# A list-scheduled attention and MLP kernel: a shift on the due date of every step, and a new set of planner constants

## The chip, the cores and the metric

One core of one Trainium2 chip runs the whole program. The metric is the device time of one execution in microseconds (us). Five engines work beside each other, each through its own instructions in order: PE (TensorE, matmuls; its weight loads are listed as PEld), DVE (VectorE), ACT (ScalarE), POOL (GpSimd) and SP (SyncE, which here issues nearly all DMAs). They wait for one another on semaphores.

## The reference

```python
for t in range(S):                       # attention: r, k, v, w are (4, 8, 768, 48), u is (8, 48)
    cur = einsum('bhd,bhe->bhde', u[None] * kt, vt)
    y[:, :, t] = einsum('bhd,bhde->bhe', rt, state + cur)
    state = wt[:, :, :, None] * state + einsum('bhd,bhe->bhde', kt, vt)
x = y.transpose(0, 2, 1, 3).reshape(3072, 384)
h = maximum(maximum(x @ w1, x @ w2), x @ w3)        # 384 -> 768
x = h @ w_out                                       # 768 -> 384
g = x @ w_gate                                      # 384 -> 1536
out = (g / (1 + exp(-g))) * (x @ w_val) @ w_out2    # 1536 -> 384
```

All of it in fp32; the weights arrive as 64-bit floats, whose words the kernel turns into fp32 itself.

## The kernel before

**Units, chunks, chains.** The attention is cut into 24 *units*: 6 chunks of 128 time steps (`c`) by 4 groups of heads (`j`, in the order 3, 0, 1, 2). A unit n goes round the engines several times. DVE makes `rk` (L478), the suffix products `I` (L418), `kh` (L421, L423), the prefix products `F` (L431) and `rp` (L434). PE then does `rk_sum` (tile `pa`, L484), the transposes of `kh` (tile `kp`, L527), `scores` (`sc`, L513), `outer` (`sc`, L609), the two parts of `y` (L553, L566) and `take_upper` (L639); the last units of chunks 0, 1 and 5 also `lend` (L539). Between them ACT copies `kp` to `khT` (L531), fills the diagonal of `A` (L499), scales the first state (L618), copies the upper half `xh` of `y` (L630) and, after `take_upper`, the lower half `xl` (L648). DVE masks `sc` into `A` (`causal`, L518) and adds to the states `s` and `S` (L622, L445). The first chunk is units 0 to 3.

**Layers.** Four finished units are one chunk of tokens (512 columns). Its first MLP is 18 `up` steps (f = 0 to 5, m = 0 to 2), each a run of nine 128x512 matmuls (L663 to L665, tile `ps`): every fp32 product is made of three matmuls with the operands split into a high and a low part. DVE takes the maximum (L768). For chunk 0 the weights are prepared just ahead: a DMA brings the 64-bit words (`raw`), DVE makes fp32 words of them in three instructions (L169 to L171), ACT rounds the high part (`hi`, L732), DVE subtracts the low part (`lo`, L737). Six `down` steps follow; in chunk 0 they are plain fp32 matmuls of the whole words (L785, `ps<-hh,whole`), each step three of them. While PE does the layers of a chunk, the next chunk's units run in between.

**Second MLP.** Twelve units of 128 hidden features (n = 0 to 11, `NU`), each for three pairs of chunks: 30 `product` steps (three matmuls of tile `px` or `py`, L973) and, laid between them, the six projections of the unit before (`proj`, tile `po`, L663 to L665 once more, nine matmuls each). Before its first low-part matmul a projection waits for `pr` from DVE (`prod_low`, L1024). All projections but the last use one PSUM tile, which has to be emptied by `collect` (L1049 on DVE, L1044 on ACT) before the next may start. `snap` (ACT, L982), `join` (DVE, L987, L989) and `mix` (POOL, L997; for k = 5 L994, on DVE in the units that `MIX5` names) combine the products; `silu` (L1004), `gate_times` (L1007) and `prod_high` (L1021) make the gated values.

**What sets the order.** Every step is entered in a `Plan` with an engine, a cost, the steps that it depends on and a due date. `Plan.order` (L72) replays the program over these costs. It pulls each due date forward to what the followers need, and then, again and again, for each engine takes the step with the smallest key among those that could start within a window `win` of the earliest start. `wt` weighs the start against the due date, `stay` favours more of the same kind; in the first 85 us of the replay fixed values stand for the three:

```python
wt, win, stay = (TUNE["wt"], TUNE["win"], TUNE["stay"]) if best > 85.0 else (15.0, 0.3, 2.0)
...
t["key"] = t["due"] + wt * t["at"] - stay * (t["kind"] == last.get(t["eng"]))
```

The sequence that comes out is what each engine gets. The second MLP's sequence on PE is fixed apart from that by `seq`: the table `GAPS` says behind which product (v, i) each of the six projections stands, and `TUNE['gaps']` which table a unit uses: the first number for most units, the second for units 4 and 8, the third for units 1 to 3. The two tables that matter here are

```python
{(0, 10): 0, (0, 13): 1, (1, 8): 2, (1, 9): 3, (1, 11): 4, (1, 13): 5},    # GAPS[2]
{(0, 11): 0, (0, 14): 1, (1, 4): 2, (1, 7): 3, (1, 10): 4, (1, 12): 5},    # GAPS[6]
```

## Time and profile before

| | us |
|---|---|
| median of 3 runs (lowest, highest) | 806.79 (805.52, 811.22) |
| the profiled execution | 805.78 |
| its span, first to last instruction | 804.0 |
| PE busy in it | 783.2 (97%) |
| DVE busy | 624.0 (78%) |
| ACT busy | 451.4 (56%) |
| POOL busy | 286.1 (36%) |

The profile is of one execution. Busy times are shares of the span. A PE matmul of 512 columns is listed with about 0.39 us, but in a stream one starts every 0.227 us or so: they overlap, and their ends are modelled. So a short wait can lie hidden in a busy PE, and the start-to-start distance shows it. In a timeline the time of a merged row runs from its start to the end of its last instruction.

### The profile page before, as it was taken

The page shows a single profiled execution, that of the slowest core. Times are in us where ns is not written, and L with a number is a line of the kernel's source. Part 1 is how long each engine was busy: PE and PEld are TensorE (multiplying, and loading weights), DVE is VectorE, ACT ScalarE, POOL GpSimd, SP SyncE. Part 2 cuts the span into 40 slices and gives each one's busy share as a digit, 9 for nine tenths or more (in the row PEclk, how much of TensorE's full clock was granted, in tenths as well). Part 3 has the DMA queues.
Part 4 walks back from the last instruction along what each step waited for, and adds up shares of the span by engine and source line. Part 5 has one row for each costly group of instructions (what it writes and reads, how often), then busy time and mean ns, then how long its engine had stood idle before and what let it go on. Part 6 is the DMA issues. An engine that isn't in the chain of part 4 may idle for free.

```text
span 804.0 us, 15834 instructions
## 1 busy us (share of the span) xinstructions
PE 783.2 (97%) x6140; PEld 638.1 (79%) x6140; DVE 624.0 (78%) x930; ACT 451.4 (56%) x983; POOL 286.1 (36%) x281
## 2 busy tenths in 40 slices
PE   6899999999999999999999999999999999999997
PEld 5777668888888888888877877878888887888885
...
GB/s 275 184 214 186 148 166 168 195 253 120 166 244 161 189 208 99 175 260 371 229 315 145 165 222 280 234 325 276 242 298 217 288 274 209 244 160 229 92 1 82
DMA packets 46482, 167.02 MB, mean 208 GB/s; under 512 B 6048, under 2 KB 11040, under 8 KB 41152
## 3 DMA queue, kind: packets, MB, share of 16 engines
...
q10 hardware_dynamic: 144, 0.13, 0.1%
...
## 4 chain that ended last, share of the span: by engine, by line
PE 88%; DVE 6%; issue 2%; POOL 1%; ACT 1%; DMA 1%; DVEq 0%; ACTq 0%
PE px L973 14%; PE py L973 13%; PE ps L663 11%; PE ps L664 10%; PE ps L665 10%; PE po L663 6%; PE po L664 6%; PE po L665 6%; PE y L553 2%; PE ps L785 2%; PE kp L527 2%; PE sc L609 2%; PE sc L513 1%; PE pa L484 1%; PE y L566 1%
## 5 line engine op out<-in xcount | busy, mean ns | idle before, releaser
L973 PE MATMUL px<-yo,W 128*128 128x512 f32 x567 | 147.6, 390 | 0.4 <-DVE sb L987 0.3
L973 PE MATMUL py<-yo,W 128*128 128x512 f32 x498 | 130.4, 389 | 0.4 <-ACT sb L982 0.4
L663 PE MATMUL ps<-xh,hi 128*128 128x512 f32 x324 | 128.9, 398 | 0.0
L664 PE MATMUL ps<-xl,hi 128*128 128x512 f32 x324 | 126.4, 390 | 0.7 <-ACT xl L648 0.5
L665 PE MATMUL ps<-xh,lo 128*128 128x512 f32 x324 | 126.4, 390 | 0.1
L997 POOL TENSOR_TENSOR sb<-sb 128x512 f32<-128x512 f32 x46 | 61.0, 1327 | 181.9 <-ACT sb L982 160.3
L973 PEld LDWEIGHTS px<-yo,W 128*128 128x128 f32 x567 | 106.2, 188 | 23.5 <-DVE sb L987 1.5
L973 PEld LDWEIGHTS py<-yo,W 128*128 128x128 f32 x498 | 93.3, 188 | 20.2 <-ACT sb L982 0.8
L987 DVE TENSOR_TENSOR sb<-px,sb 128x512 f32<-128x512 f32 x95 | 64.0, 686 | 31.8 <-PE px L973 30.4
L663 PE MATMUL po<-pr,Wp 128*128 128x512 f32 x213 | 83.6, 393 | 0.5 <-DVE acc L1049 0.2
L664 PE MATMUL po<-pr,Wp 128*128 128x512 f32 x213 | 83.2, 390 | 0.4 <-DVE pr L1024 0.4
L665 PE MATMUL po<-pr,Wp 128*128 128x512 f32 x213 | 82.9, 389 | 0.0
L1021 ACT ACTIVATE pr<-pt 128x512 fp32r<-128x512 f32 x71 | 41.9, 598 | 59.0 <-DVE pt L1007 58.0
L427 POOL COPY total<-I 128x8 f32<-128x8 f32 x24 | 11.9, 495 | 171.2 <-DVE s L445 93.0
L665 PEld LDWEIGHTS ps<-xh,lo 128*128 128x128 f32 x324 | 60.8, 188 | 13.7 <-DVE lo L737 0.5
L982 ACT ACTIVATE sb<-px 128x512 f32<-128x512 f32 x96 | 56.3, 598 | 26.8 <-PE px L973 23.9
L664 PEld LDWEIGHTS ps<-xl,hi 128*128 128x128 f32 x324 | 60.9, 188 | 12.7 <-ACT xl L648 0.8
L663 PEld LDWEIGHTS ps<-xh,hi 128*128 128x128 f32 x324 | 60.8, 188 | 12.7 <-issue 0.2
L1049 DVE TENSOR_TENSOR acc<-po,acc 128x512 f32<-128x512 f32 x53 | 36.4, 688 | 34.6 <-PE po L665 33.7
L1004 ACT ACTIVATE pt<-sb 128x512 f32<-128x512 f32 x72 | 42.6, 603 | 27.4 <-DVE pr L1024 27.3
L768 DVE TENSOR_TENSOR hw<-hw,ps 128x512 f32<-128x512 f32 x60 | 40.6, 679 | 19.9 <-PE ps L665 12.6
L989 DVE TENSOR_TENSOR sb<-sb,py 128x512 f32<-128x512 f32 x47 | 32.2, 685 | 28.3 <-ACT sb L982 25.0
...
## 6 DMA issues: line engine op xcount, KB each, us to landing
...
```

Of the source, the lines that this page charges most:

```text
L663: nc.tensor.matmul(ps, lh, rh, start=first, stop=False)
L664: nc.tensor.matmul(ps, lh, rl, start=False, stop=False)
L665: nc.tensor.matmul(ps, ll, rh, start=False, stop=last)
L768: nc.vector.tensor_tensor(hws[f], hws[f], pss[c, f, m], ALU.max)
L973: nc.tensor.matmul(X[n, v, ch], w, x, start=first and k == 0, stop=k == 2, skip_group_check=True)
L982: nc.scalar.activation(sbuf(n, v, k), X[n, v, ch], AF.Copy)
L987: nc.vector.tensor_tensor(b, X[n, v, ch], b, ALU.add)
L989: nc.vector.tensor_tensor(b, b, X[n, v, ch], ALU.subtract)
L997: nc.gpsimd.tensor_tensor(b, b, buf[n, v, "u" if k == 3 else "d"], ALU.add)
L1004: nc.scalar.activation(gated[n, k], buf[n, 0, k], AF.Silu)
L1021: nc.scalar.activation(prod[n, k][:, 0, :], gated[n, k], AF.Copy)
L1049: nc.vector.tensor_tensor(acc[a], t, acc[a], ALU.add)
```

## The change

Three tables change and one line of the planner. Every step now has a name: the function with its integer and string arguments. `SHIFT` gives a number to 666 such names, mostly steps of the weight preparation, of the second MLP and of their DMAs; `EARLIER` gives one to 201 keys of `L`: steps of units 0 to 7 and of chunk 0's layers with their weights. The shift (from -44.8 to +31.1) is added to the due date in the key by which `order` chooses; it moves no step past what it depends on, and adds or removes no instruction. `TUNE` has new values for 23 constants. Among them `mix5` (0, 3) is now (3, 11): the k = 5 mix of unit 0 goes to POOL, that of unit 11 to DVE; and `gaps` (6, 2, 3) is now (6, 6, 3): units 4 and 8 use the last of the tables instead of the third.

```diff
+SHIFT = {('w_low', 3, 0, 0): -23.8, ('product', 1, 1, 6): -11.2, ('op_high', 1, 11): 17.9, ('snap', 3, 1, 0, 'B'): -4.7,
...
+EARLIER = {('rp', 1): 6.4, ('lv', 0): 2.5, ('hl', 0, 5): -18.8, ('la', 2): 12.4, ('state1', 5): -6.5, ('scores', 7): -25.5,
...
-TUNE = {'wt': 29.41, 'win': 0.99, 'stay': 0.74, 'period': 62.0, 'soon': 14.07, 'up5': -17.12, 'check': 29.53, 'bits': -7.63,
-  'u1': 380, 'u0': 370.17, 'prep': -36.51, 'xpre': 82.52, 'xgap': 7.97, 'xafter': 11.7, 't': -8.63, 'te': 2.5, 'p1': 354.2,
-  'p2': 397.32, 'p0': 14.36, 'p3': -2.49, 'slow': (3, 5, 6, 8, 10), 'op': -11.67, 'sums': -9.09, 'mix5': (0, 3),
-  'words2': 0.75, 'gaps': (6, 2, 3), 'collect': 6.42, 'v': 2.26}
+TUNE = {'wt': 32.67, 'win': 0.89, 'stay': 1.71, 'period': 62.6, 'soon': 14.07, 'up5': -17.12, 'check': 20.84, 'bits': -9.88,
+  'u1': 377.7, 'u0': 369.84, 'prep': -37.12, 'xpre': 80.34, 'xgap': 7.97, 'xafter': 11.56, 't': -14.55, 'te': 2.5, 'p1': 357.27,
+  'p2': 423.64, 'p0': 14.27, 'p3': -10.37, 'slow': (3, 5, 6, 8, 10), 'op': -10.88, 'sums': -7.78, 'mix5': (3, 11),
+  'words2': -13.7, 'gaps': (6, 6, 3), 'collect': -5.18, 'v': 8.87}
...
-                    t["key"] = t["due"] + wt * t["at"] - stay * (t["kind"] == last.get(t["eng"]))
+                    t["key"] = t["due"] + t["shift"] + wt * t["at"] - stay * (t["kind"] == last.get(t["eng"]))
...
+    for key, d in EARLIER.items():
+        L[key]["shift"] = d
```

In the changed kernel line numbers are higher by 2 (by 4 behind L1084). Three places show what happens to the order.

PE near the start, before: from the second half of unit 0's `y` to the transposes of unit 2 (`inpA_145` is unit 2's input).

```order
L566 MATMUL y<-rp_153,s_295 48x64 x8
L513 MATMUL sc<-rp_154,kh 64x64 x16
L639 MATMUL y<-xsh,minus 128x256 x2
L609 MATMUL sc<-inpV,khT 64x48 x16
L553 MATMUL y<-A,inpV 64x64 x8
L527 MATMUL kp<-ident,kh 128x128 x4
L484 MATMUL pa<-inpA_145,rk 128x2 x4
```

And now, over the same steps:

```order
L568 MATMUL y<-rp_153,s_314 48x64 x8
L486 MATMUL pa<-inpA_145,rk 128x2 x4
L641 MATMUL y<-xsh,minus 128x256 x2
L515 MATMUL sc<-rp_154,kh 64x64 x16
L611 MATMUL sc<-inpV,khT 64x48 x16
L555 MATMUL y<-A,inpV 64x64 x8
L529 MATMUL kp<-ident,kh 128x128 x4
```

Unit 2's `pa` has moved from behind the transposes to ahead of unit 0's `take_upper` (`minus`), and unit 1's scores from ahead of it to behind it. The same happens one unit later.

DVE towards the end of chunk 0's layers, before: `hh_1113` and `hh_1256` are the hidden tiles of f = 4 and 5, `kh_1159`, `F_1163`, `rp0_153`, the states `s0_1174` and `s1_1175` and the masked `A_1151` belong to unit 6, `whole` are the words of the down weights.

```order
L421 RECIPROCAL d1f_139<-I_1073 128x8
L423 TENSOR_TENSOR kh_1159<-inpA0_143,I_1073 128x512
L431 SCALAR_TENSOR_TENSOR F_1163<-inpA0_143,d1f_139 128x520
L445 TENSOR_TENSOR s0_1174<-S1_156,total0_150 128x192
L434 TENSOR_TENSOR rp0_153<-inpA0_143,F_1163 128x512
L768 TENSOR_TENSOR hh_1113<-hh_1113,ps_1115 128x512
L622 TENSOR_TENSOR s1_1175<-s0_1174,sc_1180 128x192
L169 TENSOR_SCALAR whole_1217<-raw_1125 128x1152
L518 COPY_PREDICATED A_1151<-mask_147,sc_1180 128x512
```

And now, where `hh_1123` is the hidden tile of f = 5, `s1_898` and `S0_155` are unit 5's states, `rk_1205` is unit 7's and `kh_1208`, `F_1223` are unit 6's:

```order
L770 TENSOR_TENSOR hh_1123<-hh_1123,ps_1112 128x512
L770 TENSOR_TENSOR hh_1123<-hh_1123,ps_1140 128x512
L624 TENSOR_TENSOR s1_898<-s0_897,sc_934 128x192
L447 TENSOR_TENSOR s1_898<-s1_898,total1_151 128x192
L624 TENSOR_TENSOR S0_155<-s1_898,sc_934 128x192
L480 TENSOR_TENSOR rk_1205<-inpA1_144 128x512
L423 RECIPROCAL d1f_139<-I_1042 128x8
L425 TENSOR_TENSOR kh_1208<-inpA0_143,I_1042 128x512
L433 SCALAR_TENSOR_TENSOR F_1223<-inpA0_143,d1f_139 128x520
```

Unit 6's `kh`, `F` and `rp` now stand behind the last `hh` row, and so do its mask and states and the states of unit 5. The three instructions on the last down weights (`whole`), of which one stood behind that row, now all stand ahead of it.

PE where chunk 0's downs end and chunk 1's layers begin, before (`whole` rows are downs, the row with `hi` is the first layer matmul, `y_1399` is unit 7's `y`):

```order
L553 MATMUL y_1399<-A_1350,inpV_887 48x64 x8
L566 MATMUL y_1399<-rp1_154,s0_1329 48x64 x8
L566 MATMUL y_1399<-rp1_154,s1_1330 48x64 x8
L609 MATMUL sc_1507<-inpV_1085,khT_1462 64x48 x16
L513 MATMUL sc_1507<-rp0_153,kh_1360 64x64 x16
L527 MATMUL kp_1540<-ident_140,kh_1433 128x128 x4
L639 MATMUL y_1399<-xh_1545,minus_141 128x256 x2
L785 MATMUL ps_1458<-hh_1041,whole_1284 128x512
L785 MATMUL ps_1458<-hh_1113,whole_1284 128x512
L785 MATMUL ps_1458<-hh_1256,whole_1284 128x512
L663 MATMUL ps_1589<-xh_1087,hi_182 128x512
```

And now (`y_1355` is unit 6's `y`, `y_1458` unit 7's, `shift` its `lend`; a line of dots stands for rows left out):

```order
L787 MATMUL ps_1320<-hh_1123,whole_1127 128x512
L555 MATMUL y_1355<-A_1164,inpV_680 64x64 x8
L515 MATMUL sc_1367<-rp1_154,kh_1288 64x64 x16
...
L568 MATMUL y_1355<-rp0_153,s1_1077 48x64 x8
L529 MATMUL kp_1413<-ident_140,kh_1288 128x128 x4
L641 MATMUL y_1355<-xh_1418,minus_141 128x256 x2
L611 MATMUL sc_1367<-inpV_990,khT_1424 64x48 x16
L541 MATMUL y_1458<-xsh_987,shift_142 128x256
...
L555 MATMUL y_1458<-A_1258,inpV_990 48x64 x16
...
L568 MATMUL y_1458<-rp1_154,s1_1280 48x64 x8
...
L641 MATMUL y_1458<-xh_1513,minus_141 128x256 x2
L665 MATMUL ps_1576<-xh_1217,hi_182 128x512
```

Before, unit 7's last steps stood between downs. Now the end of unit 6 and nearly all of unit 7 stand behind the last down, with no down or layer between their steps.

## Rows read from the trace of the kernel before

**Rows 1.** Windows: us from:to, length, busy us (instructions) by engine, PEclk, DMA, GB/s.

```profile
0.00:5.80 5.80, 0.00 (x0) 0.00 (x0) 3.32 (x10) 1.90 (x3) 1.99 (x15) 1.00 0.69 219
5.80:36.50 30.70, 27.37 (x508) 24.00 (x509) 25.21 (x44) 20.19 (x72) 1.59 (x4) 1.00 0.79 224
36.50:90.70 54.20, 51.94 (x590) 40.91 (x590) 51.93 (x68) 23.00 (x51) 5.04 (x6) 1.00 0.67 205
90.70:113.30 22.60, 22.60 (x257) 12.81 (x256) 22.00 (x37) 12.33 (x35) 7.95 (x10) 1.00 0.50 136
376.00:410.00 34.00, 32.66 (x143) 26.42 (x142) 28.36 (x32) 17.59 (x34) 32.23 (x25) 1.00 0.70 253
410.00:798.00 388.00, 386.63 (x1695) 316.32 (x1693) 275.32 (x432) 240.68 (x448) 164.40 (x142) 1.00 0.62 217
798.00:804.00 6.00, 0.03 (x1) 0.00 (x0) 0.76 (x2) 0.00 (x0) 0.00 (x0) 0.89 0.22 69
```

**Rows 2.** Timeline of PE, 0 to 48 us: start, us, what [idle before <-releaser].

```profile
16.39 0.80 PE L639 MATMUL y<-xsh,minus 128*128 128x256 f32 x2 [0.20 <-ACT xsh L630]
...
19.23 0.70 PE L553 MATMUL y<-A,inpV 64*64 64x64 f32 x16 [1.01 <-DVE A L518]
...
26.09 1.86 PE L484 MATMUL pa<-inpA,rk 128*128 128x2 f32 x8
...
32.18 0.50 PE L639 MATMUL y<-xh,minus 128*128 128x256 f32 x2 [0.93 <-ACT xh L630]
...
34.83 0.44 PE L553 MATMUL y<-A,inpV 64*48 64x64 f32 x16 [0.35 <-ACT seen L579]
...
36.21 0.50 PE L639 MATMUL y<-xh,minus 128*128 128x256 f32 x2 [0.72 <-ACT xh L630]
...
37.39 0.50 PE L664 MATMUL ps<-xl,hi 128*128 128x512 f32 x1 [0.46 <-ACT xl L648]
```

**Rows 3.** Timeline of DVE, 0 to 48 and 48 to 116 us, same columns.

```profile
3.85 1.24 DVE L418 TENSOR_TENSOR_SCAN I<-inpA,d1r 128x520 f32<-128x520 f32 x1 [1.54 <-DMA inpA<-pk]
5.08 0.69 DVE L478 TENSOR_TENSOR rk<-inpA 128x512 f32<-128x512 f32 x1
...
78.06 0.65 DVE L423 TENSOR_TENSOR kh<-inpA,I 128x512 f32<-128x512 f32 x1
78.62 1.24 DVE L431 TENSOR_TENSOR_SCAN F<-inpA,d1f 128x520 f32<-128x520 f32 x1
...
80.02 0.68 DVE L434 TENSOR_TENSOR rp<-inpA,F 128x512 f32<-128x512 f32 x1
...
83.94 0.71 DVE L518 COPY_PREDICATED A<-mask,sc 128x512 f32<-128x512 uint8 x1
```

**Rows 4.** The chain that ended last, 0 to 120 us: start, us, what.

```profile
49.29 0.43 PE ps L663
49.72 0.24 PE ps L664
```

**Rows 5.** Waits of PE's weight loads: for what, us in total, times, longest.

```profile
PEld po L663 <- DVE acc L1049: 2.4, 5, 0.6
```

**Rows 6.** Timeline of PE, 528 to 548 us, at unit 4's projections.

```profile
531.09 0.40 PE L663 MATMUL po<-pr,Wp 128*128 128x512 f32 x1
531.71 0.51 PE L664 MATMUL po<-pr,Wp 128*128 128x512 f32 x1 [0.23 <-DVE pr L1024]
...
545.25 0.84 PE L973 MATMUL px<-yo,W 128*128 128x512 f32 x3
546.20 0.50 PE L663 MATMUL po<-pr,Wp 128*128 128x512 f32 x1
```

**Rows 7.** Timelines at unit 0 of the second MLP: PE, DVE and POOL.

```profile
402.98 0.96 PE L973 MATMUL py<-yo,tu 128*128 128x512 f32 x3 [1.01 <-ACT y1s L793]
...
406.66 1.73 DVE L994 TENSOR_TENSOR sb<-tr,tr 128x512 f32<-128x512 f32 x1 [1.56 <-ACT tr L982]
...
406.55 2.98 POOL L997 TENSOR_TENSOR sb<-sb,tr 128x512 f32<-128x512 f32 x2
```

14 lines of the change are left out of this document (9 added, 5 removed).

## The prediction

> **What bounds the kernel now.** I read the windows first. The profiled execution took 805.78 us, of which the span is 804.0; 1.8 us lie around it. The windows [rows 1] cut the span where the kind of work changes. PE idles 5.8 us before its first matmul and 6.0 behind its last (27.37, 51.94 and so on against the lengths give the rest): 3.3 us in the start of the first chunk (5.8 to 36.5), 2.3 in chunk 0's layers (36.5 to 90.7), none in its downs, 1.3 around the passage to the second MLP (376 to 410), 1.4 in all of the second MLP. The change adds and removes no instruction and touches neither the first load nor the last store, so 12 us of idle PE stay. About 9 us of idle time can go, and with it what is lost in PE that counts as busy: matmuls that start later than their stream would let them. All else is matmul work. That is the frame for a gain; for a loss there is none, since a worse order can hold PE up anywhere.
>
> The timeline of PE came next, for what it waits for. In the start these are hand-overs with ACT and DVE: 0.20, 1.01, 0.93, 0.35, 0.72 and 0.46 us [rows 2]. Up to some 31 us PE also runs slowly: two `minus` matmuls take 0.80 us at 16.39 and 0.50 at 32.18 [rows 2]. So in the start PE is scarce as well as waiting. In the layers of chunk 0 DVE is the second bound: it is busy 51.93 of 54.2 us and then 22.00 of 22.6 [rows 1].
>
> **The start: -1.5 us.** The order puts unit 2's `pa` ahead of unit 0's `take_upper`, and unit 3's ahead of unit 1's. A `pa` costs about 1.8 us at the slow clock (1.86) [rows 2]. It used to run when PE had other work; now it runs while ACT copies `xh` and while DVE has time to bring `rp` and the mask, which covers the 0.20 and the 1.01. I walked both orders from the first matmul with the durations of the trace. Up to unit 0's `y` they are level (unit 1's `pa` is only swapped with scores and `outer`; that DVE now begins with `rk`, for which the second half of the input must have landed, costs nothing as long as that happens by the 5.1 us at which `rk` ran before [rows 3]). At unit 1's first `y` the new order is half a microsecond later, but one `pa` of 1.8 us further. Against that, DVE now has unit 3's `kh` and `rk` and five operations on weight words ahead of unit 2's `rp`, so the scores of unit 2 wait some 0.3 us. By the first layer matmul, 36.5 us before [rows 1], I get 35.0: 1.5 of the 3.3 us of idle time gone. Bounds: the whole 3.3 gone; or `rk` first makes everything 1.2 us late (the scan started at 3.85 and would now start behind 5.1 [rows 3]) and nothing is covered.
>
> **Layers and downs of chunk 0: -1.3 us.** Three terms. First, DVE has less to do ahead of the last maximum: unit 6's `kh`, `F`, `rp` and mask are deferred, 0.65 + 1.24 + 0.68 + 0.71 = 3.3 us [rows 3]; the deferred state operations and the `whole` operation that came forward about balance. Scores also stand several layer steps ahead of the `y` that needs their mask. I take it that the 2.3 us of waits [rows 1] go. Second, the layer matmuls are interrupted less: they stand in 10 runs instead of 15, the downs in 3 instead of 5. The first matmul of a run takes 0.43 us of the chain, the following ones 0.24 [rows 4]. That is 0.19 us for each of 5 runs, and about as much for one of the downs' two: 1.2. Third, what was deferred has to be paid: the end of unit 6 and all of unit 7 now run behind the last down, one step waiting for another, with nothing of the layers to fill in. Unit 3 shows the price, as it too ended without fillers: in its last steps, up to the second layer matmul at 37.39, PE waited 0.35 + 0.72 + 0.46 = 1.5 us [rows 2]. Unit 7 has about the same, and the take and `outer` of unit 6 about 0.7 more: 2.2. Sum 2.3 + 1.2 - 2.2 = 1.3. Bounds: a gain of 3.5 if units 6 and 7 fill each other's waits, a loss as in the slower rival. What would be late next is DVE: it stays busy behind the downs with what was put off, and its first operation of unit 7's mask cannot start before that unit's scores.
>
> **The passage at 400 us: +0.4.** What is gained up to here arrives earlier at a stretch where POOL is busy 32.23 of 34 us [rows 1] and where PE's wait of 1.01 us is for an ACT copy (`y1s`) that stands behind the rounding of projection weights [rows 7]. In the new order it still does. These weights come by a DMA that waits for a buffer, which waits for POOL's sums. Since POOL's own chain begins with results of PE and DVE, I expect most of an earlier start to reach it, and put 0.4 of the 2.8 us down as lost; bounds 0 and all 2.8.
>
> **Unit 0's mix moves to POOL: +0.6.** On DVE the k = 5 mix ended at 408.4 (406.66 + 1.73); two mixes on POOL beside it took 2.98, so 1.49 each [rows 7]. In the new order POOL does the k = 3 mix first and the k = 5 mix second, which ends at 406.55 + 2.98 = 409.5: 1.1 us later, behind it the join on which PE waits. POOL's queue ahead of it is a little shifted, and DVE is relieved; I take half, 0.6 (bounds 0 and 1.1). Unit 11's mix in exchange moves to DVE, which has room there (0).
>
> **The projections of units 4 and 8: -1.5.** Their table put the third and the fourth projection one product apart, and there is one PSUM tile. So PE waits until `collect` has emptied it: behind the three matmuls at 545.25, which start 0.227 apart ((0.84 - 0.39) / 2, with 0.39 for a single one), the next projection should start at 545.93 and starts at 546.20, and its first matmul takes 0.50 instead of 0.39: 0.38 lost [rows 6]. The new table leaves at least two products between any two. It also moves the first projection one product (0.68 us) on. At 531.71 a matmul waits for `pr` and comes 0.62 behind its predecessor instead of 0.23, and takes 0.11 longer: 0.5 lost [rows 6]; the one before it lost about as much. I take it that one of these two goes (0.46) and one stays in part. Unit 8 has two waits of the `collect` kind; five of these sum to 2.4 us of idle weight loads [rows 5], 0.48 each, which by the case above is some 0.33 of lost matmul time. 0.38 + 0.46 + 2 x 0.33 = 1.5. Bounds 0 (the later projections push `collect` and `pr` into each other) and 2.1.
>
> For the other moves I put nothing: the sequence of products is fixed, their waits in the second MLP are small [rows 1], and the order leaves the largest of the remaining ones as it was (two low-part subtractions of weights still stand ahead of one `collect` in unit 2). New waits of that size are possible; 1 us either way goes into the range.
>
> **Sum.** -1.5 - 1.3 + 0.4 + 0.6 - 1.5 = -3.3, from 805.8: 802.5 us. The profiled execution is 1.0 below the median of the three runs (806.79), so a median of the new kernel could read up to a microsecond more.
>
> **Rivals.** *The clock rises sooner.* The granted clock reads 1.00 in every window [rows 1], yet `minus` runs at nearly half speed until about 31 us [rows 2], which is the lower of TensorE's two levels (1.2 and 2.4 GHz). PE was idle for 1.01 us at 18.2, then worked without a break for 12 us, and was at full speed afterwards. The new order fills that gap. If the rise came at 20 instead of 31 us, 11 us of PE work would shrink by 5; ACT's and DVE's hand-overs would take back about half. That is 3 us more: 799.5. The Trainium skill says in "TensorE: Matmul & The Clock Gate" (Part 1) that the throttled state is the default and that activity releases it, which fits a sooner rise; that a full 25 us of these small matmuls did not release it speaks against counting on it.
>
> *The gain of the start is lost at 400.* If POOL's chain there ends when it ended before, only the last two terms are left: 805.8 + 0.6 - 1.5 = 804.9. For it speaks the POOL row, against it that POOL, too, waits for DVE at the beginning of that stretch.
>
> *Slower: units 6 and 7 are exposed.* The place is PE behind the last down. If each of the two units passes its hand-overs one by one (`kp` to `khT`, scores to mask, `xh`, `xl`: some 0.6 to 0.7 us each, 2.6 a unit) that is 5.2 instead of 2.2, and if DVE, with 0.6 us of room in the downs [rows 1], cannot take the 3.3 us put off there, 2.7 more are waited for: 7.9 against 2.3 + 1.2 + 1.5 won. With the mix at its worst (1.1) and the projections' gain eaten by new waits: 805.8 + 7.9 - 5.0 + 1.1 = 809.8. It decides itself from the point where chunk 1's first layer matmul starts later than 113.3 us. Against it speaks that all downs, 16 us of PE work, give DVE time for unit 6 before.
>
> **Chances.** The forecast's case (801 to 804) 0.5; sooner clock or stalls gone further 0.17; lost at 400 0.18; slower 0.15. The range is 798.0 to 808.5, which leaves out some 0.18. A measurement of this kernel tells about 1% (8 us) from no change. Faster by more than that needs the sooner clock on top of nearly all bounds: 0.11. Slower by more, above 814.9, needs more than the slower rival: 0.05. Within 1%: 0.84.
>
> **What would show it.** In the new trace the first `xh,hi` matmul should start near 35.0 us and chunk 1's first near 110.5 (113.3 before); PE idle in the windows of the start and the layers about 1.8 and 0, with 2 us between the last down and chunk 1; at unit 4 no wait for `acc`. Wrong is the forecast if that first matmul of chunk 1 is later than 113.3, if the wait for `y1s` at 400 has grown by the amount won, or if waits of PE in the second MLP add up to more than before.

## The result and the profile after

The changed kernel takes 812.98 us (median of 12 runs, 811.63 to 819.6), the kernel before, run beside it, 807.89 (12 runs, 804.1 to 811.22). The ratio is 1.0071, interval [1.0047, 1.0095]: slower, by less than the 1% that I took as telling. The forecast was 802.5, its range 798.0 to 808.5: the sign is wrong and the result lies outside the range.

One thing has to be known for all that follows. The profiled execution of before took 805.78, a second one of it 805.69; its median over all runs on record lies near 808. Both profiled executions of after (812.79 and 812.80) lie at its median. So two profiles differ by 7.0 us where the medians differ by 5.1. No profile shows where before's other executions spend their 2 us more; what the record has on it stands under "What stays open".

Windows of after, cut where the kind of work changes as in [rows 1] (us from:to, length, busy us (instructions) of PE, PEld, DVE, ACT, POOL, then PEclk, DMA share, GB/s):

```profile
5.88:40.15 34.27, 29.80 (x509) 25.98 (x509) 30.75 (x49) 20.60 (x73) 2.01 (x5) 1.00 0.75 209
40.15:107.80 67.65, 66.94 (x568) 47.96 (x568) 62.56 (x81) 26.31 (x61) 8.79 (x10) 1.00 0.64 188
107.80:115.81 8.01, 7.41 (x277) 6.45 (x277) 7.92 (x11) 5.59 (x17) 7.04 (x7) 1.00 0.39 110
115.81:404.65 288.84, 286.53 (x3063) 237.84 (x3061) 241.02 (x346) 150.02 (x374) 93.52 (x96) 1.00 0.64 200
404.65:804.62 399.97, 395.46 (x1731) 322.96 (x1729) 280.05 (x437) 247.58 (x459) 175.99 (x150) 1.00 0.61 217
```

The start lasts 34.27 us where it lasted 30.70 [rows 1]. PE idles 4.47 us in it instead of 3.33, and its 509 matmuls (508 in before's row) are busy for 29.80 instead of 27.37. Layers and downs of chunk 0, with the tail behind the last down (third row), take 75.66 instead of 76.80, so part comes back. The rest of the loss lies behind 115 us. In the second MLP (last row) PE idles 4.5 us; over the same stretch of before (399.76 to 798.00) it idles 2.7. That is one of the signs by which the prediction said it would be wrong; that chunk 1 begins later than 113.3 us is another.

The start on PE (start, us, what, x count, [idle before <-releaser]), to set beside [rows 2]:

```profile
13.32 0.71 PE L555 MATMUL y<-A,inpV 64*64 64x64 f32 x16 [0.91 <-DVE A L520]
...
21.49 0.80 PE L555 MATMUL y<-A,inpV 64*64 64x64 f32 x16 [0.93 <-DVE A L520]
...
29.94 0.71 PE L555 MATMUL y<-A,inpV 64*64 64x64 f32 x16 [0.93 <-DVE A L520]
...
39.55 0.79 PE L641 MATMUL y<-xh,minus 128*128 128x256 f32 x2 [0.72 <-ACT xh L632]
40.15 0.63 PE L665 MATMUL ps<-xh,hi 128*128 128x512 f32 x1
...
41.03 0.79 PE L666 MATMUL ps<-xl,hi 128*128 128x512 f32 x1 [0.26 <-ACT xl L650]
...
43.20 0.40 PE L665 MATMUL ps<-xh,hi 128*128 128x512 f32 x1
```

The 1.01 us for one unit's mask has become three waits of 0.91, 0.93 and 0.93. And `minus` still takes 0.79 at 39.55, where before it took 0.50 from 32.18 on: PE is at the lower of its two levels until 43 us, when a 512-column matmul falls from 0.63 to 0.40.

What the mask waits for is in DVE's timeline:

```profile
20.62 0.72 DVE L520 COPY_PREDICATED A<-mask,sc 128x512 f32<-128x512 uint8 x1 [0.89 <-PE sc L611]
```

DVE is idle too: it waits for PE's `outer` (L611), because `outer` writes the same tile `sc` as the scores that are masked. So behind scores and `outer` PE has 0.9 us with nothing but the mask to wait for, unless a step stands there that needs no mask. In before such a step stood there for units 0 and 2. PE's timeline of before, unit 0, from `outer` to the first `y`:

```profile
9.60 1.11 PE L609 MATMUL sc<-inpV,khT 64*64 64x48 f32 x32
10.63 1.86 PE L484 MATMUL pa<-inpA,rk 128*128 128x2 f32 x8
12.52 0.71 PE L553 MATMUL y<-A,inpV 64*64 64x64 f32 x16
```

The `pa` is unit 1's, and `y` follows it without a wait. In after this `pa` stands ahead of unit 0's scores, the next two ahead of `take_upper`, and `y` waits each time.

In chunks 1 to 5 one kind of wait has grown. PE, ACT and DVE around 150 us:

```profile
153.02 0.46 PE L555 MATMUL y<-A,inpV 64*64 64x64 f32 x16 [1.70 <-ACT seen L581]
```

```profile
151.79 0.63 ACT L775 ACTIVATE hh<-hw 128x512 fp32r<-128x512 f32 x1 [3.62 <-DVE hw L770]
152.33 0.58 ACT L768 ACTIVATE hw<-ps 128x512 f32<-128x512 f32 x1
152.81 0.16 ACT L581 ACTIVATE seen<-y 128x2 f32<-128x2 f32 x1
```

```profile
147.40 2.05 DVE L433 TENSOR_TENSOR_SCAN F<-inpA,d1f 128x520 f32<-128x520 f32 x1
...
149.95 1.23 DVE L420 TENSOR_TENSOR_SCAN I<-inpA,d1r 128x520 f32<-128x520 f32 x1
151.10 0.66 DVE L770 TENSOR_TENSOR hw<-hw,ps 128x512 f32<-128x512 f32 x1
```

PE waits 1.70 us for a copy of 0.16 us (`seen`, a small copy out of `y` at L581). The copy is third in ACT's queue behind `hh`, the rounded hidden tile, and `hh` waits 3.62 us for DVE's last maximum of that step, which stands behind two scans. Over the whole program (waits of PE's weight loads: total, times, longest) this kind takes 3.9 us in after (2.7 in a second execution), against 1.3 us in three waits before (first row):

```profile
PEld y L553 <- ACT seen L579: 1.3, 3, 0.5
PEld y L555 <- ACT seen L581: 3.9, 6, 1.8
PEld po L665 <- DVE acc L1051: 2.6, 4, 0.9
```

The last row answers to [rows 5]: 2.6 us in four waits instead of 2.4 in five. The waits for `acc` have not gone; those of units 4 and 8 have given way to two in unit 3.

Unit 0 of the second MLP, PE, POOL and DVE, beside [rows 7]:

```profile
407.07 0.96 PE L975 MATMUL py<-yo,tu 128*128 128x512 f32 x3 [0.22 <-ACT y1s L795]
...
415.67 0.96 PE L975 MATMUL px<-yo,W 128*128 128x512 f32 x3 [2.19 <-DVE sb L989]
```

```profile
412.37 1.30 POOL L999 TENSOR_TENSOR sb<-sb,tr 128x512 f32<-128x512 f32 x1
413.61 1.27 POOL L996 TENSOR_TENSOR sb<-tr,tr 128x512 f32<-128x512 f32 x1
```

```profile
414.92 1.29 DVE L989 TENSOR_TENSOR sb<-px,sb 128x512 f32<-128x512 f32 x2 [1.39 <-POOL sb L996]
```

The wait for `y1s` is down from 1.01 to 0.22. Another of 2.19 stands in its place: PE waits for the join, the join for POOL's k = 5 mix, and that mix is second in POOL's queue, behind the k = 3 mix.

Units 3 and 4, PE and DVE, beside [rows 6]:

```profile
522.12 0.50 PE L665 MATMUL po<-pr,Wp 128*128 128x512 f32 x1 [0.52 <-DVE acc L1051]
...
526.25 0.50 PE L665 MATMUL po<-pr,Wp 128*128 128x512 f32 x1 [0.44 <-DVE acc L1051]
...
539.92 0.50 PE L666 MATMUL po<-pr,Wp 128*128 128x512 f32 x1 [0.83 <-DVE pr L1026]
```

```profile
518.84 2.62 DVE L874 TENSOR_TENSOR yo<-xr,yo 128x512 fp32r<-128x512 f32 x2
521.38 0.68 DVE L1051 TENSOR_TENSOR acc<-po,acc 128x512 f32<-128x512 f32 x1
...
524.93 0.67 DVE L874 TENSOR_TENSOR yo<-y,yo 128x512 fp32r<-128x512 f32 x1
525.52 0.68 DVE L1051 TENSOR_TENSOR acc<-po,acc 128x512 f32<-128x512 f32 x1
```

In unit 3 a `collect` (L1051) that PE waits for stands behind low parts of weights (`yo`, L874). Unit 4 has no wait for `acc` any more, but one of 0.83 for `pr`.

### The profile page after: what moved, and what is told of

It reads as the page before. It is cut to its first block, busy times and chain, and to the rows that moved or that the text cites. A ratio compares the mean times of both kernels' runs of the same rounds, so it can differ in the third digit from the quotient of the medians.

```text
span 811.0 us, 15818 instructions
## 1 busy us (share of the span) xinstructions
PE 786.1 (97%) x6140; PEld 641.2 (79%) x6140; DVE 625.1 (77%) x930; ACT 451.7 (56%) x983; POOL 288.7 (36%) x281
## 4 chain that ended last, share of the span: by engine, by line
PE 81%; DVE 6%; POOL 4%; DMA 4%; ACT 2%; issue 2%; SPq 0%; DVEq 0%; POOLq 0%; ACTq 0%
PE px L975 15%; PE py L975 13%; PE ps L665 9%; PE ps L666 9%; PE ps L667 9%; PE po L665 6%; PE po L666 6%; PE po L667 6%; DMA inpA<-pk 2%; PE ps L787 2%; PE y L555 2%; PE kp L529 1%; PE sc L515 1%; PE sc L611 1%; POOL st L916 1%
## 5 line engine op out<-in xcount | busy, mean ns | idle before, releaser
L1051 DVE TENSOR_TENSOR acc<-po,acc 128x512 f32<-128x512 f32 x53 | 36.5, 688 | 38.0 <-PE po L667 36.7
L429 POOL COPY total<-I 128x8 f32<-128x8 f32 x24 | 10.1, 421 | 142.4 <-DVE I L420 70.4
L468 POOL TENSOR_TENSOR inpT<-inpT,uB 128x192 f32<-128x192 f32 x32 | 26.8, 858 | 92.4 <-DMA inpT<-pk 76.4
```

What stands on the lines that cost most here:

```text
L468: nc.gpsimd.tensor_tensor(q, q, uu, ALU.mult)
L1051: nc.vector.tensor_tensor(acc[a], t, acc[a], ALU.add)
```

## The experiments

**How they are compared.** Each run's time stands with its run. This table cuts the profiled executions at fixed points of the program, in us. *Start* is from the program's first instruction to the first layer matmul of chunk 0, taken as 0.23 before the second, `ps<-xl,hi` (by that count the first layer matmul is at 37.16 in before, not at the 36.5 at which its row begins, because the second waits; the expectations' numbers for it are on this count). *Busy* and *idle* are PE's from its first matmul (of the kernel's own work) to that point. *Chunk 0* reaches from there to the same point of chunk 1, *chunks 1-5* to the first product of the second MLP. Units are those of the second MLP, from first product to first product, 0.227 us for each matmul of a merged row ahead of it.

| execution | start | busy | idle | chunk 0 | chunks 1-5 | unit 0 | unit 3 | unit 4 | unit 8 |
|---|---|---|---|---|---|---|---|---|---|
| before | 37.16 | 27.80 | 3.54 | 75.99 | 286.61 | 22.33 | 33.14 | 34.08 | 33.45 |
| before_again | 36.50 | 25.38 | 5.21 | 77.05 | 286.57 | 21.32 | 33.12 | 34.07 | 33.40 |
| warm_before | 37.64 | 28.43 | 3.57 | 77.15 | 286.12 | 21.15 | 33.11 | 34.10 | 33.44 |
| before_gaps | 38.49 | 29.05 | 3.81 | 77.47 | 286.47 | 21.34 | 33.12 | 35.66 | 33.38 |
| before_rk | 37.99 | 27.75 | 4.49 | 76.80 | 287.88 | 21.42 | 33.12 | 34.12 | 33.42 |
| after | 40.80 | 30.43 | 4.49 | 75.02 | 288.83 | 23.73 | 34.66 | 33.84 | 32.80 |
| after_again | 41.09 | 30.70 | 4.60 | 76.56 | 287.40 | 23.79 | 34.68 | 33.85 | 32.81 |
| no_shift | 39.55 | 28.29 | 5.06 | 77.36 | 288.34 | 23.43 | 34.68 | 33.33 | 32.89 |
| start_back | 37.56 | 27.51 | 4.17 | 80.05 | 287.29 | 23.72 | 34.68 | 33.86 | 32.79 |
| mixgaps_back | 39.26 | 28.63 | 4.90 | 76.78 | 286.55 | 24.78 | 34.98 | 40.01 | 34.10 |
| no_earlier | 37.93 | 28.36 | 3.59 | 76.40 | 288.12 | 23.08 | 33.58 | 39.27 | 33.85 |
| earlier_only | 41.91 | 30.80 | 5.48 | 78.15 | 288.41 | 27.00 | 34.45 | 33.63 | 33.44 |
| three_swaps | 41.35 | 30.86 | 4.85 | 77.30 | 285.81 | 21.90 | 34.18 | 33.84 | 32.81 |
| swaps_fill | 39.20 | 27.57 | 5.96 | 81.76 | 285.81 | 22.84 | 34.18 | 33.84 | 32.81 |
| swaps_all | 41.20 | 28.76 | 6.79 | 79.66 | 285.79 | 22.54 | 34.22 | 33.84 | 32.79 |

Stages of one order repeat to some tenths from unit 3 on; start, chunk 0 and chunks 1-5 scatter by 1 to 3 us, so for these I go by several executions. Part of the scatter in the first two is PE's level. It changes up to seven times before 60 us, and not at the same times in two executions of one kernel.

### The start alone, the clock alone

**start_back**: after, with `EARLIER` left off for the steps of attention units 0 to 3.

```diff
-        L[key]["shift"] = d
+        if key[0] not in UNIT_KEYS or key[1] > 3:
+            L[key]["shift"] = d
```

> The changed kernel, but EARLIER is applied only to keys of units 4 to 7 and of chunk 0's layers and weights; the first four units are ordered as in the kernel before. Nothing else in the order differs behind chunk 0. Theory A (the start loses 3.6 us because the moved pa uncovers DVE's mask, PE never works long enough without a gap, and it stays at the slow level until 43 instead of 31 us): minus of unit 2 runs in 0.50 us near 32.2, the first layer matmul is back at 36.5, chunk 1's first layer matmul comes near 112.4 instead of 115.8, and the time is about 809.2 (3.6 below the changed kernel's 812.8). Rival (the layers of chunk 0 are bound by DVE and would give any earlier start back): first layer matmul at 36.5, but chunk 1's still near 115.8 and the time near 812.8.

Measured: 812.99 us (12 runs), ratio 1.0054 [1.0029, 1.0080], as after. The start is back at 37.56 us, 3.2 less than in after. But chunk 0 takes 80.05 instead of 75.02. PE's timeline:

```profile
91.98 0.63 PE L530 MATMUL kp<-ident,kh 128*128 128x128 f32 x4 [1.34 <-DVE kh L426]
```

An earlier start ran into DVE: this `kh`, and two waits of 0.46 and 0.20 us for a weight's `lo` before it. But that is the smaller part. Of the 5.0 us by which chunk 0 is longer than in after, PE idles 1.6 and is busy 3.4 more (77.18 us against 73.74), with the same matmuls. The granted clock shows why: it is 0.50 from 28.4 to 42.0 us, so the first 4.4 us of layers ran at the lower level (2.2 us of them in after), and once more behind the wait for `kh`:

```profile
93.30:96.70 3.40, 3.40 (x38) 2.26 (x39) 2.95 (x8) 2.74 (x10) 0.19 (x1) 0.50 0.50 125
```

So chunk 0 gave the earlier start back, about one third by waits for DVE and two thirds by PE's level. The start of the new order is 3 us longer, but putting it right alone is worth nothing.

**warm_before** and **warm_after**: before and after, each with nine matmuls ahead of the first step whose result nothing reads. They ask what PE's level costs.

```diff
+        warm = mm([128, 512], "warm")
+        for _ in range(9):
+            nc.tensor.matmul(warm, d1r[:, 0:128], d1r[:, 0:512], start=True, stop=True)
```

> The kernel before with the same nine matmuls. If the clock is what counts in the start, PE's 25 us of slow work shrinks, but DVE (24 us busy in it) and the hand-overs take over: first layer matmul at 32 to 34 us instead of 36.5, time 803 to 805 in place of 807.9 (some 3 to 4 less). If the clock falls again during the small matmuls, or PE's speed does not matter beside DVE: first layer matmul 36 to 37, time within 1 us of the kernel before.

> The changed kernel with nine extra bf16 matmuls of 512 columns on constants, results unused, ahead of unit 0, while PE waits for the first input (about 1.9 to 5.8 us). Theory A1 (the loss of the start is mostly the clock): minus of unit 0 takes 0.50 us or less instead of 0.77, the first layer matmul comes at 36 us or sooner instead of 40.15, and the time falls by 4 us or more, to 809 or less. Rival A2 (the loss is the waits for the mask, three of 0.9 us): the waits stay or grow, the first layer matmul stays within 1 us of 40, time 812 to 813. Third: the small matmuls of the units do not hold the clock and it falls again by the first minus; then nothing changes.

Measured: warm_before 805.06 us (12 runs, 802.33 to 806.65), ratio 0.9957 [0.9936, 0.9978], faster than both kernels. warm_after 814.97 (10 runs), 1.0079 [1.0052, 1.0105], no gain. In warm_before the nine matmuls did not raise the level at once; PE's timeline and a window:

```profile
1.79 4.02 PE L1642 MATMUL warm<-d1r 128*128 128x512 bf16 x9 [1.79 <-DVE d1r L362]
5.64 1.87 PE L484 MATMUL pa<-inpA,rk 128*128 128x2 f32 x8
...
19.97 0.95 PE L484 MATMUL pa<-inpA,rk 128*128 128x2 f32 x8
...
24.53 1.86 PE L484 MATMUL pa<-inpA,rk 128*128 128x2 f32 x8
```

```profile
24.00:30.00 6.00, 5.69 (x116) 5.05 (x110) 4.54 (x10) 4.26 (x18) 0.00 (x0) 0.50 0.73 181
```

PE was fast near 20 us, then slow again, and the start took 37.64. The profile of warm_before has no stage that is clearly shorter than before's, and the profiled executions took the same (805.77 and 805.78). Its gain is in the medians; which stage it comes from is open.

### The tables

**mixgaps_back**: after, with the two constants as before.

```diff
-  'mix5': (3, 11),
+  'mix5': (0, 3),
...
-  'gaps': (6, 6, 3),
+  'gaps': (6, 2, 3),
```

> The changed kernel with mix5 (0, 3) and gaps (6, 2, 3) as before; the order differs from the changed kernel's only in the second MLP. Theory B (unit 0's k=5 mix on POOL costs PE the wait of 2.19 us at 415.7, and the new table costs unit 4 more than it gives unit 8): that wait falls to 0.3 to 0.5 (1.8 gained), unit 4's waits fall back from 0.52 + 0.44 + 0.83 to about 0.6 (1.4 gained), unit 8 loses 0.6: about 810.2 in place of 812.8. Rival (the table as such gains what was forecast, and unit 4's waits come from the shifts of collect and prod_low): unit 4's waits stay, unit 8 loses 1, and the time is about 812.

Measured: 819.97 us (6 runs), 1.0143 [1.0106, 1.0180]. Unit 4 takes 6.2 us more than in after, unit 8 1.3 more; and unit 0, with the k = 5 mix on DVE again, 24.78. DVE and PE:

```profile
408.40 2.52 DVE L996 TENSOR_TENSOR sb<-tr,tr 128x512 f32<-128x512 f32 x1 [1.57 <-ACT tr L984]
```

```profile
538.65 0.50 PE L666 MATMUL po<-pr,Wp 128*128 128x512 f32 x1 [1.65 <-DVE pr L1026]
...
542.00 0.50 PE L665 MATMUL po<-pr,Wp 128*128 128x512 f32 x1 [2.62 <-ACT pr L1023]
```

The mix that I charged at 1.73 for DVE [rows 7] took 2.52 here. POOL was at work beside it both times, there on two mixes, here first on an operation on projection weights (L954, 2.67 us). So leaving the mix on DVE would have cost as much as the move to POOL; what can be saved is the place in POOL's queue (three_swaps, below).

**before_gaps**: before, with `gaps` (6, 6, 3) and nothing else.

> The kernel before with gaps (6, 6, 3) alone: units 4 and 8 use the changed kernel's table, nothing is shifted. Term of the forecast: 1.5 gained, unit 4 33.1 us instead of 34.08 and unit 8 32.8 instead of 33.45; 806.5 in place of 808.0. What the changed kernel's trace showed: 0.24 and 0.65, 807.1. Rival (table and due dates only go together, as the changed kernel with the old table lost 6 us in unit 4): unit 4 35 us or more, 809 or more.

Measured: 809.11 us (11 runs), 1.0010 [0.9982, 1.0037]. Unit 8 stayed (33.38), and unit 4 took 1.58 more, 35.66, with a wait for `pr` of 1.03 us and on PE:

```profile
532.53 0.96 PE L973 MATMUL px<-yo,W 128*128 128x512 f32 x3 [1.40 <-DVE sb L987]
```

The same table loses where the order around it is the old one, and the old table loses in the new order. Table and order go together; neither has a price of its own.

**no_earlier** (after without `EARLIER`), **earlier_only** (before with `EARLIER` alone) and **no_shift** (after with `SHIFT` empty):

```diff
-    for key, d in EARLIER.items():
-        L[key]["shift"] = d
```

```diff
-SHIFT = {('w_low', 3, 0, 0): -23.8, ('product', 1, 1, 6): -11.2,
...
+SHIFT = {}
```

> The changed kernel without EARLIER: SHIFT and the new constants stay, the shifts of units 0 to 7 and of chunk 0's layers are gone. Theory S (the start's order is what costs, 2 to 3.6 us, and the chain of waits it sets off in chunks 1 to 5 another 1.7; the second MLP costs 1.7): first layer matmul near 37.2, chunk 1's first layer matmul to the first product 286.4 us as before, the second MLP 1.7 longer than before; time about 809.7. Rival M (the constants and SHIFT alone put the stall into chunks 1 to 5): 288 us there, time about 811.5.

> The kernel before with EARLIER alone: no SHIFT, the old constants. Theory S: first layer matmul near 40, chunk 1's first 2 to 3 us later than before, 1 to 3 us more between it and the first product, the second MLP as before (398.3 from the first product to the last matmul): time 810.5 to 812. Rival M: the first half as before but for the start, which chunk 0's layers give back: 808 to 809.

> The changed kernel without SHIFT (EARLIER and the new constants stay). PE's order is the changed kernel's to the last instruction; DVE, ACT, POOL and SP differ in the second MLP. Theory: the waits of unit 3 (34.66 us) and unit 0 (23.7) come from SHIFT: unit 3 33.1, unit 0 22.3 to 23, all else as the changed kernel, time 810. Rival: SHIFT is what makes the new table fit (unit 4 33.84, unit 8 32.80), as no_earlier's and mixgaps_back's 39 and 40 us of unit 4 hint: without it unit 4 takes 35 us or more, time 814 or more.

Measured: no_earlier 813.58 us (11 runs), 1.0059 [1.0034, 1.0083]; earlier_only 820.84 (5 runs), 1.0146 [1.0099, 1.0193]; no_shift 813.13 (11 runs), 1.0067 [1.0046, 1.0087]. `SHIFT` alone is worth nothing that can be measured. `EARLIER` costs the start (41.91 with it alone, 37.93 without it), and its effect does not end with chunk 0, since the replay plans everything behind it anew: without it unit 4 took 39.27 instead of 33.84. With it alone PE met a single wait at 415 us:

```profile
415.37 1.14 PE L975 MATMUL py<-yo,tu 128*128 128x512 f32 x3 [4.71 <-ACT y1s L795]
```

### Local repairs behind the start

**three_swaps**: after, with the list that the planner returns edited in three kinds of places: in chunks 1 to 5 ACT's `hh` (and what needs it) behind `seen`, in ten places; in unit 3 two `collect` ahead of a low part on DVE; in unit 0 the k = 5 mix ahead of the k = 3 mix on POOL. `behind(a, b)` puts step a, and what needs it, behind b.

```diff
+        for g in [o for o in steps if o["name"] and o["name"][0] == "group" and o["name"][1] > BLOCK]:
+            late = [o for o in on_engine(g, "ACT", 4.0) if o["name"] and o["name"][0] == "hidden"]
...
+        for turn in (15, 16):
+            c = L["collect", turn]
+            o = on_engine(c, "DVE", 4.0)[-1]
+            if o["name"][0] == "op_low":
+                behind(o, c)
+        behind(L["mix", 0, 0, 3], L["mix", 0, 0, 5])
```

> The changed kernel with three kinds of neighbours swapped, nothing else: in chunks 1 to 5 ACT copies seen before the hh that waits for DVE (ten places), in the second MLP's unit 3 DVE does collect before the low part yo (two places), in unit 0 POOL does the k=5 mix before the k=3 mix. Theory: each names the cause of a wait. Chunks 1 to 5 take 286.3 us instead of 288.8 (no wait for seen over 0.3 but the one at the end of chunk 5's units), unit 3 33.15 us instead of 34.66 (its waits for acc of 0.52 and 0.44 gone), unit 0 22.7 instead of 23.7 (the join starts 1.2 sooner): together some 4 us, 809. Rival: DVE and POOL are late as a whole, the waits move to the next step: chunks 1 to 5 above 288, unit 3 above 34, unit 0 above 23.4; time 812.

Measured: 809.51 us (11 runs), ratio to before 1.0014 [0.9990, 1.0038]: 3.5 less than after. ACT and PE:

```profile
153.07 0.17 ACT L581 ACTIVATE seen<-y 128x2 f32<-128x2 f32 x1 [1.86 <-PE y L555]
153.14 0.62 ACT L775 ACTIVATE hh<-hw 128x512 fp32r<-128x512 f32 x1
```

```profile
413.65 0.96 PE L975 MATMUL px<-yo,W 128*128 128x512 f32 x3 [0.87 <-DVE sb L989]
...
523.79 0.50 PE L665 MATMUL po<-pr,Wp 128*128 128x512 f32 x1 [0.77 <-DVE acc L1051]
```

`seen` now waits for PE and no longer for `hh`. Chunks 1-5 took 285.8 in this and every later kernel with the edit, 1.6 to 3.0 less than in the two executions of after. The wait in unit 0 fell from 2.19 to 0.87, the unit to 21.90. Unit 3 gained 0.5 of its 1.5: one wait went, the other grew from 0.44 to 0.77. So for chunks 1 to 5 and for unit 0 the cause is shown by taking it away, for unit 3 a third of it; there another low part (1.68 us at 520.86) still stands two steps ahead of the second `collect`. The kernel as a whole is no longer told from before, although its start is as long as after's.

**warm_seen**: warm_before with `seen` ahead of `hh`.

> The kernel before with the nine matmuls ahead of unit 0 (as in warm_before, 805.1) and with seen ahead of hh on ACT in chunks 1 to 5 (as in three_swaps). Both effects are real and add up: chunks 1 to 5 285.8 instead of 286.4, time 804.5. Rival: the gain of warm_before (3 us, which none of its stages shows) was chance: time 807 to 808.

Measured: 805.73 us (12 runs), 0.9971 [0.9951, 0.9991]. Not told apart from warm_before; it bears out that the nine matmuls help the order before.

### Which step of the start

All of these build on three_swaps, so that what they change is the start.

**swaps_pa** puts `pa` of attention units 1 to 3 behind the `outer` of the unit before; **swaps_rk** puts unit 0's `rk` behind its `I`, unit 1's behind unit 0's `rp`; **swaps_both** is both; **swaps_all** puts besides the scores of units 1 and 2 ahead of the `take_upper` of the unit before. **swaps_fill** leaves the order and adds two matmuls that nothing reads ahead of the first `y` of units 0 to 2, where PE waits for the mask. **before_rk** is before with unit 0's `rk` ahead of its `I`.

```diff
+        behind(L["take", 0], L["scores", 1])
+        behind(L["take", 1], L["scores", 2])
+        behind(L["rk", 0], L["suffix", 0])
+        behind(L["rk", 1], L["rp", 0])
+        for n in (1, 2, 3):
+            behind(L["rk_sum", n], L["outer", n - 1])
...
```

```diff
+        for _ in range(2 * (n < 3)):
+            nc.tensor.matmul(ys[n][:, 0, :], d1r[:, 0:128], d1r[:, 0:512], start=True, stop=True, skip_group_check=True)
```

> The kernel three_swaps, and in the start pa of units 1, 2 and 3 stands again behind the outer of the unit before, with the copies that follow it on ACT; scores, take_upper and everything on DVE, POOL and SP stay as in the changed kernel. Theory S1 (the move of pa is what costs in the start: it uncovers the mask, three waits of 0.9 us): the waits for A at about 14 and 30 us go, first layer matmul (the one with xl, 41.0 to 42.1 us in the changed order, 37.2 to 38.5 in the old one) at 38.5 or sooner; if the layers of chunk 0 keep it, 807. Rival S2 (it is the order of DVE, rk first, and of scores and take_upper): within 0.7 of 41. Rival S3 (the layers of chunk 0 give it back, as in start_back): first layer matmul sooner, chunk 1's still near 118, time 809 to 810.

> The kernel three_swaps with two of DVE's steps back in their old places: rk of unit 0 behind the scan I, rk of unit 1 behind rp of unit 0. PE's order stays. Theory D (the scan waits for the second half of the first load because rk stands ahead of it, and each hand-over behind it comes later): I starts at 3.9 instead of 5.75, unit 0's rp ends near 8.4 instead of 10.3, PE's first scores start near 8.8 to 9.6 instead of 10.4, and the first layer matmul (its xl part; 41.35 in three_swaps, 39.3 to 41.9 in the executions of this order) comes 1.3 to 2 us sooner than three_swaps': 39.4 to 40; time 808. Rival E (PE's order and its later mask waits set the start, DVE has time): first scores sooner, first layer matmul still 40.6 to 42, time 809.5 to 811.

> The kernel three_swaps with both: pa of units 1 to 3 behind the outer of the unit before (swaps_pa) and DVE's rk behind the scan I of unit 0 and behind its rp (swaps_rk). Theory P (either moved alone leaves a wait that the other covers: pa behind outer covers the mask, the early rp lets scores start): the waits for A at 13.6 and 30 us and the wait of scores for rp of 1.44 us are gone, the xl part of the first layer matmul comes at 38 to 39.5, time 807. Rival Q (scores and take_upper in their new order, or the loads, set the pace): 40.5 or later, time 809 to 811.

> The kernel swaps_both, and scores of units 1 and 2 stand ahead of take_upper of the unit before again. Theory W (each unit has two hand-overs to wait for, xh and the mask, some 1 us each, and two pieces of PE work that can stand in them, scores and pa; the old order puts one into each, the new one puts pa into the first and lets scores stand where it covers nothing): the two waits of 1.05 us at 16 and 24 us shrink to 0.2 to 0.3, the xl part of the first layer matmul comes at 38 to 39 instead of 40.83, and with the second MLP as in three_swaps the time is 806 to 807. Rival: the loads or DVE's later steps set the pace of units 2 and 3: 40 or later, 808.5.

> The kernel three_swaps with two useless bf16 matmuls of 512 columns ahead of the first y of units 0, 1 and 2, where PE waits 0.9 us for the mask. They lie in the wait. Theory C (PE's gaps keep it at the slow level in the start): without the gaps it reaches the fast level before 30 us (minus 0.50 us, not 0.80) and the first layer matmul comes 1 to 2 us sooner, at 39.5 instead of 41.3; time 808. Rival: the level comes and goes on its own: minus 0.80 at 26 and 33 us, first layer matmul at 40.5 to 42, time 809 to 810.

> The kernel before with one pair swapped on DVE: rk of unit 0 ahead of its scan I. Theory D: the scan starts at 5.75 instead of 3.85, unit 0's rp ends near 9.6 instead of 8.3, and the first layer matmul's xl part comes 1 to 1.9 us later than 37.2 to 38.5: near 39; time 809 to 809.5. The forecast's own view (rk first costs nothing): 37.2 to 38.5, time 808.

| kernel | us (runs) | ratio to before | start | busy | idle |
|---|---|---|---|---|---|
| swaps_pa | 811.37 (11) | 1.0038 [1.0014, 1.0062] | 42.91 | 30.81 | 6.07 |
| swaps_rk | 809.66 (11) | 1.0011 [0.9990, 1.0032] | 41.13 | 30.67 | 4.74 |
| swaps_both | 808.71 (11) | 1.0015 [0.9996, 1.0033] | 40.83 | 30.78 | 4.44 |
| swaps_all | 811.56 (12) | 1.0043 [1.0022, 1.0064] | 41.20 | 28.76 | 6.79 |
| swaps_fill | 811.93 (11) | 1.0042 [1.0021, 1.0063] | 39.20 | 27.57 | 5.96 |
| before_rk | 808.02 (11) | 1.0001 [0.9980, 1.0023] | 37.99 | 27.75 | 4.49 |

No partial undoing brought the start back; only the whole old order did (start_back, no_earlier). swaps_pa covers the mask again: its three waits for `A` are gone. But others stand in their place, 1.44 us for unit 0's `rp` and 1.05, 1.05 and 0.64 for `xh`, and the start is the longest of all. So the uncovered mask alone is not what the new start costs. swaps_both has little more waiting than the old order (4.44 us against 3.5 to 5.2); there the rest is PE's level, the lower one throughout. In swaps_all it is the waiting again. PE and DVE:

```profile
17.19 1.13 PE L515 MATMUL sc<-rp,kh 64*64 64x64 f32 x32 [2.12 <-DVE rp L436]
```

```profile
16.36 0.69 DVE L436 TENSOR_TENSOR rp<-inpA,F 128x512 f32<-128x512 f32 x1
```

With PE's order put right, PE waits 2.12 us for unit 1's `rp`, which DVE makes behind unit 2's `rk`, `I` and `kh`. PE's new order is fitted to DVE's new order. `rk` first alone does not cost measurable time: before_rk measures 808.02. Its start is 0.8 us later than in the two executions of the old order whose clock rose when its did (37.99 against 37.16 in before and 37.13 in warm_seen; the rise came at 31 to 32 us in all three), with new waits of 0.18 us for `kh` and 0.70 for `rp`.

swaps_fill tells the clock from the order. PE:

```profile
16.50 1.02 PE L486 MATMUL pa<-inpA,rk 128*128 128x2 f32 x8
17.39 0.48 PE L643 MATMUL y<-xsh,minus 128*128 128x256 f32 x2
19.10 0.95 PE L515 MATMUL sc<-rp,kh 64*64 64x64 f32 x32 [1.23 <-DVE rp L436]
...
27.36 1.14 PE L515 MATMUL sc<-rp,kh 64*64 64x64 f32 x32 [1.61 <-DVE rp L436]
```

PE is at the upper level at 16.5 us: `pa` takes 1.02 instead of 1.86. It does not stay there. The granted clock reads 1.00 from 16.0 to 19.3 us, 0.50 up to 22.7, 1.00 up to 26.2 and 0.50 up to 33.0, and the scores at 27.36 take 1.14 again. The start shrinks by 2.2 us against three_swaps, but stays above all executions in the old order, as the waits for `rp` grow to 1.23 and 1.61. Chunk 0 then took 81.76 and gave it back, 2.5 us by more busy time and 2.0 by waiting (78.22 and 3.54 us against 75.75 and 1.55 in three_swaps).

**before_again**, **after_again**: one more profile of each kernel, unchanged.

> The kernel before once more, for its stages: if the gain of warm_before lies in one stage, this execution is longer there than warm_before's (start and layers of chunk 0 up to chunk 1's first layer matmul 114.8, chunks 1 to 5 286.1, unit 0 21.2, rest 376.1); otherwise the 2 to 3 us are spread.

> The changed kernel once more: first layer matmul (xl part) 39.2 to 42, chunk 0's layers and downs 75 to 78.5, chunks 1 to 5 286.5 to 290 with waits for seen, unit 0 23.7, unit 3 34.66, unit 4 33.84, unit 8 32.80 (the last three the same to 0.05 in each execution of this order so far).

They took 805.69 and 812.80 us. They bear out the difference of the two profiles. The start came out within 0.7 us of the first profile for each kernel; over all executions of an order it spreads by 2 to 2.7 us. And before_again reached its like start another way: PE was fast from 16.8 to 27.0 us, slow until 40.6, and waited more (5.21 us against 3.54).

## Why the prediction was wrong

**The start: -1.5 forecast, +3 measured.** Two sentences failed. "Up to unit 0's `y` they are level (unit 1's `pa` is only swapped with scores and `outer`)": that swap took the cover off unit 0's mask. And that `pa`, now run while ACT copies `xh`, "covers the 0.20 and the 1.01": it covers the 0.20 (and the scores ahead of `minus` cover unit 2's 0.93), but the 1.01 was the wait for unit 1's mask behind `outer`, and in the new order no `pa` stands behind any `outer`. One wait of that kind became three. What the prediction nowhere counts is that the mask is made only when `outer` is done, whose matmuls go into the same tile. That names where the new order waits, not what it costs: swaps_pa put `pa` back behind `outer`, and the start grew to 42.91, since DVE's order was changed with PE's. The eight executions in the old order (five in the table, warm_seen, start_back and no_earlier) have on the mean 27.8 us busy and 4.0 idle in the start, the six in the new one without an edit to it (after, after_again, no_shift, mixgaps_back, earlier_only, three_swaps) 30.0 and 4.9. That is 0.9 more waiting, and 2.2 more for the same 509 matmuls. But a faster PE also waits more, so the two are not separate prices. At like busy time (28.29 and 28.63 in no_shift and mixgaps_back, 28.36 and 28.43 in no_earlier and warm_before) busy and idle make 33.4 us in the new order and 32.0 in the old: 1.4 for the order, the other half for PE's level. This split is an estimate from four executions. "That DVE now begins with `rk` ... costs nothing" held for the time of the kernel; the start by itself lost 0.8 us by it in the old order (before_rk), and in the new one it was covered (41.13 in swaps_rk, 41.35 in three_swaps).

**The clock rises sooner: the rival went the other way.** Its argument was that the new order fills PE's gap at 18 us. There are three gaps now, and in four of those six executions PE stayed at its lower level throughout (busy 30.4 or more), while every execution in the old order had a fast stretch. The Trainium skill, "TensorE: Matmul & The Clock Gate" (Part 1), says that activity releases the throttled state. swaps_fill agrees in part: with two extra matmuls at each of three places PE was fast at 16.5 us, and it was slow again at 19.4. warm_before, where PE fell back by 24.53 with the old order's work behind it, also shows that it doesn't last by itself; and before_again was fast at 16.8 us with nothing added. What makes the old order reach the upper level more often is not settled.

**Chunk 0: -1.3 forecast, 0 measured.** In the profile the term looks right: 75.66 against 76.80 us, idle 1.3 instead of 2.3, and the stretch behind the last down, for which I put 2.2 us of waiting, has 0.6, as unit 8's scores and `outer` stand between unit 7's last steps. The gain of 1.2 for fewer interruptions (1.1 by its own numbers) doesn't show there (busy 74.35 against 74.54), but PE ran at the lower level for the first 2.9 us of after's stage and not at all in before's. And over executions the stage is level: 76.9 on the mean of the six in the new order, and 76.9 of the six in the old one that have the old chunk 0 as well. The step that failed is that the 2.3 us of waits go: over these executions PE is busy 74.8 us in the new order and 75.3 in the old, but idle 2.0 and 1.6. mixgaps_back shows it best, as it has the new order here and PE was at the upper level throughout, as in before: busy 73.62 us against 73.95, idle 3.16 against 2.04 (1.33 of it one wait for a mask), so 0.8 longer. With the start put right (start_back) the stage took 80.05, for the two reasons given there. The slower rival's mechanism, units 6 and 7 exposed, did not happen, though the time came out beyond its 809.8: chunk 1 begins at 115.81, later than the 113.3 that it named, from the start and not from the tail.

**Chunks 1 to 5: no term, +0.8 to 2.2 measured.** I took everything behind chunk 0 as moved but not changed. The waits for `seen` grew from 1.3 to 3.9 us in after's profile and to 2.7 in after_again's; three_swaps removes the cause, and the stage is then shorter than in before (285.81 against 286.61).

**Passage and unit 0: +1.0 forecast, +1.4 to 2.5 measured.** PE did not come earlier to `y1s` but 4.9 us later, and that wait shrank by 0.8, so the +0.4 for the passage fell away. For the mix my bound was 1.1. Counted from the unit's first product it ends 1.6 us later than before (414.88 - 404.65 against 408.39 - 399.76), and PE reaches the join 0.8 sooner because of `y1s`: 2.4 together, and the wait there grew by 1.9, from 0.33 to 2.19. So the mechanism was right (the k = 5 mix second in POOL's queue), the size was off, since what a shorter wait gives PE is added to the next. Turning the two mixes round takes 1.3 of it away. The 1.73 on DVE that I compared with is 2.52 in mixgaps_back, so staying on DVE would not have been better.

**Unit 3: nothing forecast, +1.5 measured.** The prediction said that new waits of this size were possible, "1 us either way". It named two low parts ahead of a `collect` in unit 2; the same stands in unit 3 now, where PE waited for none of that size before.

**Units 4 and 8: -1.5 forecast, -0.9 measured.** Unit 8 gave 0.65 for 0.66. Unit 4 gave 0.24 for 0.84: the waits for `acc` went, as forecast, but the `pr` wait that I took as half gone is 0.83 at 539.92. before_gaps shows that the table as such is not the cause of either gain, since alone it makes unit 4 longer by 1.58.

**Sum.** Of the 7.0 us between the two profiles the start has 3.6, chunk 0 -1.0, chunks 1-5 2.2, unit 0 1.4, units 1 and 2 -0.5, unit 3 1.5, unit 4 -0.2, unit 8 -0.65, what is left 0.6. The forecast had priced the places that the change improves. The losses behind the start are at places where a step that nobody had waited for came to stand ahead of one that somebody waits for; in the start that is about half, and the other half is PE's level.

**What stays open.** Where before's typical run spends 2 us more than its profiled ones, and so where warm_before gains its 3. The granted clock of the runs points at PE's level: of the 142 runs of before beside the experiments, the 52 with a mean clock of 0.983 to 0.987 have a median of 808.4 us, the 31 with 0.989 to 0.992 one of 806.5, and the two profiled executions read 0.999 and 0.990. That they go together is not yet a cause. Which of DVE's moves in the start costs most: an edit that also brings unit 1's `rp` forward on DVE was not tried. And what the start costs in the end: no run has the old start and the three swaps together. three_swaps, which has the new start, lies 0.1% above before, with an interval from -0.1% to 0.4%, so this can be anything up to 3 us.
